# Attention with a gated MLP on one core: the second projection unit of a block placed in the middle of its values unit

## The chip, the cores and the metric

The kernel runs on one NeuronCore of a Trainium2 chip. The metric is the device time of one execution in microseconds (us), as the median of several runs.

## The reference

A layer norm of x (2048 x 640) feeds two branches. The attention branch has 32 heads of width 192 with a K and a V cache of 2048 keys. The other branch is a SwiGLU MLP. The result is x + attention * silu(MLP).

```python
xn = layernorm(x)
q  = (xn @ wq) -> 32 heads of 192
p  = softmax(q @ k_cache.T * 192 ** -0.5)
s  = (p @ v_cache) -> 2048 x 6144, @ wo
g  = silu((silu(xn @ w1) * (xn @ w3)) @ w2)
return x + s * g
```

## The kernel before

Attention ends at 1675 us of the 1976 us profiled. It is a stream of steps. A head has four blocks of 512 queries (`qb`), and a block has eight steps (`p`), each over a pair of 128-key tiles. In each step TensorE does two units of work:

- A scores unit, for the step two ahead: six matmuls of 64 rows and 512 columns, in three pairs: one matmul on the first 64 rows and one on the other 64, which start 20 ns apart in the trace. ACT then takes the exp of the 128 x 1024 result.
- A values unit, for this step: sixteen matmuls of 64 rows and 193 columns, eight pairs, that multiply the exp of two steps ago with V and sum into two output banks.

In two of the eight steps a projection unit for the next head is put in: ten matmuls of 64 rows and 512 columns, five pairs, with a copy on ACT and an add on DVE behind them. The first one (`half` 1, weights `wqB`) stands in step 0, the second one (`half` 0, weights `wq`) in step 4. In head 0, which also computes the layer norm, they stand in steps 5 and 7.

What the argument turns on is PSUM. Scores units and projection units take their output from the same pool, which has two buffers; the output banks have a pool of their own. So each new scores or projection unit needs the buffer of the unit before the last one to have been read.

```python
ps_st = main.enter_context(tc.tile_pool(name="ps_st", bufs=2, space=bass.MemoryType.PSUM))
# ... cut ...
    def project(h, qb, half):
        # ... cut: tiles of the destination ...
        w = L["wqB"] if half else L["wq"]
        ps = ps_st.tile([P, 1024], F32, tag="st2", name="ps")
        # ... cut: head 0 ...
            for c in range(DC):
                for r in range(2):
                    rows = slice(r * 64, (r + 1) * 64)
                    nc.tensor.matmul(ps[:, r * 512:(r + 1) * 512], lhsT=w[rows, c, 0:P], rhs=xnT[rows, c, qs],
                                     start=(c == 0), stop=(c == DC - 1))
            part = hbp.tile([P, 512], F32, tag="part", name="part")
            nc.scalar.copy(out=part[:], in_=ps[:, 0:512])
            nc.vector.tensor_tensor(out=dst, in0=ps[:, 512:1024], in1=part[:], op=ALU.add)
# ... cut ...
    def emit_scores(h, qb, p):
        # ... cut ...
        st2 = ps_st.tile([P, 1024], F32, tag="st2", name="st2")
        # ... cut: three rounds of two matmuls into st2 ...
        pT2 = pp.tile([P, 1024], BF16, tag="pT2", name="pT2")
        nc.scalar.activation(out=pT2[:], in_=st2[:], func=ACT.Exp, scale=att_scale)
# ... cut ...
    for n, (h, qb, p) in enumerate(stream):
        scores(n + 2)
        if h + 1 < H and p == (5 if h == 0 else 0):
            project(h + 1, qb, 1)
        if h + 1 < H and p == (NPAIR - 1 if h == 0 else NPAIR // 2):
            project(h + 1, qb, 0)
        values(n)
        if p == 0 and n > 0:
            finish_block(n - 1)
        if p == (6 if h == 0 else 2) and h < 2 * NPIG:
            swiglu(h, qb)          # even heads: a tanh on ACT and work on DVE; odd heads: DVE alone
```

## Time and profile before

| | before |
|---|---|
| time, median of 3 runs | 1978.36 us |
| TensorE matmul busy | 1952.1 us, 99% of the profiled span |
| ScalarE (ACT) busy | 67% |
| an ordinary step (scores and values) | 1.31 us |
| last score pair to second projection, even heads (64 blocks), median | 360 ns from start to start |
| the same, odd heads (60 blocks), median | 253 ns |
| the same, if nothing waited | 216 ns |

The medians stand for nearly all blocks: four of the even ones, those of head 0, have 267 or 268 ns, two have 530, and one odd block has 216. The second and third rows are from the profile's page. These are its lines of busy time, of the granted clock by slices (in tenths, 9 being 90% or more), and the chain of work that ended last:

```profile
PE 1952.1 (99%) x27311; PEld 1386.0 (70%) x27311; DVE 738.3 (37%) x1109; ACT 1319.6 (67%) x1525; POOL 333.2 (17%) x570
...
PEclk9999999999999999999999999999999999999999
...
PE 96%; ACT 2%; DVE 1%; DMA 1%; issue 0%; ACTq 0%
```

This says that TensorE bounds the kernel, and it seems to say that it never waits. The list of waits agrees on the face of it. It gives the idle time on an engine, who ended it, the total in us, the number of times and the longest:

```profile
PE obank L395 <- ACT osum L405: 2.9, 7, 0.6
...
PE ps L319 <- ACT pT L369: 0.2, 1, 0.2
```

By this list a projection (`ps`, L319) waited for an exp (`pT`, L369) once, for 0.2 us. L319 is the line of both projections. The page's groups of instructions keep them apart (busy us and mean ns of one, then the idle us before them and who ended it):

```profile
L319 PE MATMUL ps<-xnT,wq 64*128 64x512 bf16 x1240 | 155.7, 376 | 0.3
L319 PE MATMUL ps<-xnT,wqB 64*128 64x512 bf16 x1240 | 155.7, 376 | 0.2 <-ACT pT L369 0.2
```

So that one wait belongs to the first projection (`wqB`), and for the second (`wq`) the profile names no wait at all. But a matmul's end is modelled. The Trainium skill, "Perfetto Trace Analysis", Tensor Engine Instruction, says that the profiler estimates it from the instruction's size. Here each 64 x 512 matmul is shown as 376 ns long, while such pairs start 216 ns apart when nothing holds them up. So a wait of up to 160 ns (180 ns after the second matmul of a pair, which starts 20 ns later) lies under the tail of the matmul before it and counts as busy. One has to read starts instead. This is the timeline of the kernel before around one second projection, in an even head (start in us, length in us, engine, source line, operation, tiles, shapes; in brackets the engine's idle time just before):

```profile
804.97 0.62 ACT L345 ACTIVATE pt<-qAB 64x512 bf16<-64x512 bf16 x1
...
805.49 1.00 ACT L369 ACTIVATE pT<-st 128x1024 bf16<-128x1024 f32 x1
...
806.19 0.38 PE L366 MATMUL st<-qC,KC 64*128 64x512 bf16 x1
...
806.55 1.26 PE L319 MATMUL ps<-xnT,wq 64*128 64x512 bf16 x10
...
807.62 0.85 PE L395 MATMUL obank<-vt,pT 64*128 64x193 bf16 x16
807.84 0.58 ACT L322 COPY part<-ps 128x512 f32<-128x512 f32 x1
...
808.46 0.69 DVE L323 TENSOR_TENSOR qAB<-ps,part 128x512 bf16<-128x512 f32 x1 [2.15 <-ACT part L322]
...
809.61 0.38 PE L366 MATMUL st<-qAB,KA 64*128 64x512 bf16 x1
```

The last score pair starts at 806.19 and the projection at 806.55: 360 ns in place of 216. The exp of the scores before (L369) ran from 805.49 to 806.49, and the projection starts just after its end. The distance is 51 or 52 ns in 123 of the 124 blocks, worked out from the starts and lengths in the trace; in the other block nothing waited. The exp is late because the SwiGLU step's tanh (L345, 0.62 us) went ahead of it on ACT. That tanh exists in even heads only. In odd heads the same reading gives 253 ns, again 52 ns after the exp's end, as in this block:

```profile
754.09 1.02 ACT L369 ACTIVATE pT<-st 128x1024 bf16<-128x1024 f32 x1 [0.29 <-PE st L367]
...
754.91 0.38 PE L366 MATMUL st<-qC,KC 64*128 64x512 bf16 x1
...
755.16 1.26 PE L319 MATMUL ps<-xnT,wq 64*128 64x512 bf16 x10
```

The last two lines of the even head's timeline matter for what the change could cost. The projection's buffer is free when the add on DVE is done, at 808.46 + 0.69 = 809.15, and the scores unit that takes it next starts at 809.61, with 455 ns to spare.

### The profile page before, as it was taken

Reading aid. Unit: us, or ns where it says so; the run is one execution under the profiler, and the core shown is the slowest. Engines: PE = TensorE matmul, PEld = TensorE weight load, DVE = VectorE, ACT = ScalarE, POOL = GpSimd, SP = SyncE. Lnnn points to the kernel's source line nnn. Section 1 sums busy time; section 2 is a strip of 40 time slices with the busy share of each in tenths; the row PEclk is TensorE's granted clock in tenths of the full one; section 3 lists DMA queues with packets and bytes.
Section 4 is the critical chain, followed back from the end, with each engine's and each line's share of the span. In section 5 each row is a group of like instructions: output and inputs, shape, how many; then the busy total and the mean of one; then the engine's idle time right before and its main releaser. Section 6 shows DMA issues by size and latency. Waiting matters only on the chain.

```text
span 1976.3 us, 60169 instructions
## 1 busy us (share of the span) xinstructions
PE 1952.1 (99%) x27311; PEld 1386.0 (70%) x27311; DVE 738.3 (37%) x1109; ACT 1319.6 (67%) x1525; POOL 333.2 (17%) x570
## 2 busy tenths in 40 slices
PE   7999999999999999999999999999999999999998
PEld 5677777777777777777777777777777776577776
DVE  5433434333344443334333333443433333521111
ACT  4677787777777777777777777777778777210000
POOL 2222112112221221122122112212211210000000
PEclk9999999999999999999999999999999999999999
DMA  6223233334333434363334343433323230928883
GB/s 153 56 56 91 62 100 66 95 67 100 69 98 69 101 69 99 69 167 67 100 69 101 67 101 69 87 80 73 91 58 92 62 80 4 263 37 150 151 143 70
DMA packets 359718, 177.96 MB, mean 90 GB/s; under 512 B 305552, under 2 KB 346256, under 8 KB 359456
## 3 DMA queue, kind: packets, MB, share of 16 engines
q1 hardware_dynamic: 331824, 113.92, 27.4%
q0 software_dynamic: 23120, 56.72, 11.6%
q8 instruction: 215, 3.52, 0.8%
q10 hardware_dynamic: 4512, 3.41, 0.6%
q14 instruction: 47, 0.39, 0.1%
HBM read 55.44 MB, written 27.79 MB: 42 GB/s over the span
## 4 chain that ended last, share of the span: by engine, by line
PE 96%; ACT 2%; DVE 1%; DMA 1%; issue 0%; ACTq 0%
PE obank L395 34%; PE st L366 30%; PE ps L319 14%; PE ps_s L106 11%; PE st L367 3%; PE ps_f L560 3%; PE ps_gu L531 1%; PE ps_gu L534 1%; ACT pT L369 1%; DMA vt<-in_A_k_cache_dram 1%; PE ps L312 0%; DVE stats L275 0%; ACT osum L405 0%; PE pst L291 0%; ACT xnT L294 0%
## 5 line engine op out<-in xcount | busy, mean ns | idle before, releaser
L369 ACT ACTIVATE pT<-st 128x1024 bf16<-128x1024 f32 x1024 | 1048.9, 1024 | 347.4 <-PE st L367 347.3
L395 PEld LDWEIGHTS <-pT 64*128 64x128 bf16 x16384 | 745.6, 94 | 215.0 <-issue 7.7
L395 PE MATMUL obank<-vt,pT 64*128 64x193 bf16 x16384 | 867.1, 243 | 5.2 <-ACT osum L405 2.9
L366 PE MATMUL st<-qAB,KA 64*128 64x512 bf16 x1024 | 385.1, 376 | 1.6 <-ACT pT L369 0.9
L366 PE MATMUL st<-qC,KC 64*128 64x512 bf16 x1024 | 385.0, 376 | 0.8 <-DVE KC L244 0.8
L366 PE MATMUL st<-qC,KB 64*128 64x512 bf16 x1024 | 385.0, 376 | 0.2 <-ACT qC L329 0.2
L367 PE MATMUL st<-qAB,KA 64*128 64x512 bf16 x1024 | 385.1, 376 | 0.0
L367 PE MATMUL st<-qC,KC 64*128 64x512 bf16 x1024 | 385.0, 376 | 0.0
L367 PE MATMUL st<-qAB,KB 64*128 64x512 bf16 x1024 | 385.0, 376 | 0.0
L332 POOL DMA_DIRECT2D qC<-qAB x254 | 134.4, 529 | 1250.3 <-DVE rl_all L413 654.8
L323 DVE TENSOR_TENSOR qAB<-ps,part 128x512 bf16<-128x512 f32 x248 | 171.4, 691 | 421.8 <-ACT part L322 420.9
L406 DVE COPY opart<-obank 128x772 f32<-128x772 f32 x128 | 123.0, 961 | 425.4 <-PE obank L395 425.4
L106 PE MATMUL ps_s<-wo_sb,oT 128*128 128x256 bf16 (+3 forms) x1536 | 208.8, 299 | 0.0
L106 PEld LDWEIGHTS <-oT 128*128 128x128 bf16 x1536 | 148.4, 98 | 60.4
L366 PEld LDWEIGHTS <-KC 64*128 64x128 bf16 x1024 | 96.2, 94 | 105.1 <-DVE KC L244 1.1
L319 PE MATMUL ps<-xnT,wq 64*128 64x512 bf16 x1240 | 155.7, 376 | 0.3
L319 PE MATMUL ps<-xnT,wqB 64*128 64x512 bf16 x1240 | 155.7, 376 | 0.2 <-ACT pT L369 0.2
L322 ACT COPY part<-ps 128x512 f32<-128x512 f32 x248 | 147.7, 596 | 10.7 <-PE ps L319 0.9
L407 DVE TENSOR_TENSOR osum<-osum,opart 128x772 f32<-128x772 f32 x128 | 123.2, 963 | 21.3 <-ACT osum L405 20.8
L414 DVE TENSOR_TENSOR ostage<-osum,rl_all 128x768 bf16<-128x768 f32 x128 | 122.6, 958 | 4.4
L319 PEld LDWEIGHTS <-wq 64*128 64x128 bf16 x1240 | 67.2, 94 | 77.6 <-issue 26.4
L319 PEld LDWEIGHTS <-wqB 64*128 64x128 bf16 x1240 | 67.2, 94 | 71.4 <-issue 20.0
(75 smaller groups left out, 1263.3 us busy)
## 6 DMA issues: line engine op xcount, KB each, us to landing
vt<-in_A_v_cache_dram SPq DMA_DIRECT2D x32, 768.0 KB, 6.6
o_scr<-ostage SPq DMA_DIRECT2D x16, 1536.0 KB, 8.9
qC<-qAB POOLq DMA_DIRECT2D x381, 64.0 KB, 1.9
wq<-in_A_wq_dram POOLq DMA_DIRECT2D x32, 240.0 KB, 3.5
wo_sb<-in_A_wo_dram POOLq DMA_DIRECT2D x1, 7680.0 KB, 38.5
KC<-KA POOLq DMA_DIRECT2D x31, 128.0 KB, 4.8
KC<-KB POOLq DMA_DIRECT2D x31, 128.0 KB, 5.9
x_all<-in_A_x_dram SPq DMA_DIRECT2D x4, 640.0 KB, 9.3
```

The costliest lines, as they stand in the source:

```text
L106: nc.tensor.matmul(ps[:, 0:w], lhsT=oT[:, k, :], rhs=wo_sb[:, k, c0:c1], start=(k == 0), stop=(k == OC - 1))
L319: nc.tensor.matmul(ps[:, r * 512:(r + 1) * 512], lhsT=w[rows, c, 0:P], rhs=xnT[rows, c, qs], start=(c == 0), stop=(c == DC - 1))
L322: nc.scalar.copy(out=part[:], in_=ps[:, 0:512])
L323: nc.vector.tensor_tensor(out=dst, in0=ps[:, 512:1024], in1=part[:], op=ALU.add)
L332: nc.gpsimd.dma_start(out=qC[0:64, half, qs], in_=qAB[64:P, half, qs])
L366: nc.tensor.matmul(st2[:, 0:512], lhsT=k0, rhs=q0, start=r == 0, stop=r == 2)
L367: nc.tensor.matmul(st2[:, 512:1024], lhsT=k1, rhs=q1, start=r == 0, stop=r == 2)
L369: nc.scalar.activation(out=pT2[:], in_=st2[:], func=ACT.Exp, scale=att_scale)
L395: nc.tensor.matmul(obanks[r][:, j * 256:j * 256 + DH + 1], lhsT=pT2[r * 64:(r + 1) * 64, t * 512 + j * P:t * 512 + (j + 1) * P], rhs=vt[r ...
L406: nc.vector.tensor_copy(out=opart[:], in_=ov[1])
L407: nc.vector.tensor_tensor(out=osum[:], in0=osum[:], in1=opart[:], op=ALU.add)
L414: nc.vector.tensor_tensor(out=ostage[:, qb * 4:qb * 4 + 4, hg * DH:(hg + 1) * DH], in0=osum[:, :, 0:DH], in1=rl.unsqueeze(2).to_broadcast( ...
```

## The change

The intent is to let the second projection unit come later, so that its buffer is free when its turn comes, and to fill the time with half of the values unit, which was ready long before.

```diff
-    def values(n):
+    def values(n, between=None):
@@
         for t in range(2):
+            if t == 1 and between is not None:
+                between()
             for j in range(4):
@@
         if h + 1 < H and p == (NPAIR - 1 if h == 0 else NPAIR // 2):
-            project(h + 1, qb, 0)
-        values(n)
+            values(n, between=lambda: project(h + 1, qb, 0))
+        else:
+            values(n)
```

No instruction is added or removed. In 124 blocks (31 heads of four) eight value matmuls go ahead of the ten projection matmuls. The order on the other engines is the same.

## The prediction

> **What bounds the kernel.** TensorE. The busy table has PE at 99% of the 1976.3 us span, the chain of waits is 96% PE, and the granted clock is full in every slice. But matmul ends are modelled (the Trainium skill, "Perfetto Trace Analysis", Tensor Engine Instruction: the end is an estimate): a 64x512 matmul is shown as 376 ns, while in the timeline such pairs start 215 ns apart. So waits of up to 160 ns are hidden inside "busy", and I read starts instead.
>
> An ordinary step (six score, sixteen value matmuls) takes 1.31 us in the timeline, with a steady 216 ns from the last score pair to the values and 83 ns from one value pair to the next: no waits. At the second projection unit (the one on the plain weights wq) it is not steady. From the last score pair to the first projection pair the starts lie 360 ns apart in 64 of the 124 blocks (even heads) and 253 ns in 60 (odd heads), mean 308, where 216 would be back to back. In every block looked at the projection starts 52 ns after the end of the exp of the step before (806.49 to 806.55 us in one). That is its PSUM wait: scores and projection alternate between two buffers, and the projection needs the one that this exp is reading. In even heads the exp is later because a tanh (0.62 us on ACT) went before it. Matmuls stay in program order, so nothing else runs meanwhile (the Trainium skill, "TensorE: Matmul & The Clock Gate", Part 2, step 1; the trace agrees).
>
> **What the change does.** No instruction is added or removed. Eight value matmuls, ready long before, go in front of the ten projection matmuls; eight stay behind. They take 4 x 83 = 332 ns, so the projection comes no sooner than 548 ns after the last score pair, while its buffer is free at about 360 ns (even) or 253 (odd). The wait goes away.
>
> **Worth.** (308 - 216) ns x 124 = 11.4 us, all of it on PE's chain. The first projection unit (253 ns, 37 ns lost in each of 124 blocks, 4.6 us) is not touched and keeps its wait.
>
> **What could be given back.** The projection ends later against the scores behind it. Its buffer is freed by an ACT copy and a DVE add that end 1.72 us after its last matmul starts. The second scores unit after it takes that buffer; today it starts 455 ns after the add's end. With half the values moved ahead I work out 1.84 us from last projection matmul to that scores unit: 120 ns after the add's end, about 70 after a release of 50. Tight, but it should not wait.  So I expect nothing back.
>
> **Prediction.** 1978.36 - 11.2 = 1967.2 us, range 1965.6 to 1971.0. Within 2%: 0.99.
>
> **What would show it.** Right: in the timeline the first projection pair starts 83 ns after the fourth value pair, in even and odd heads alike; the second values half follows 216 ns after the last projection pair; the first projection unit still shows 253 ns. PE busy falls by about the saving, since the waits were counted as busy.
>
> **What would make it wrong.** If the second scores unit after the projection does wait for the add: each 50 ns there costs 6 us. If changing from 193-column to 512-column matmuls in the middle of the values costs a bubble.

## The result, and the profile after

The changed kernel took 1967.90 us in the median of 4 runs (1967.58 to 1967.97), against 1978.34 us before (the median of 4 runs of its own). That is 10.4 us less: clear of the spread of the runs. The ratio is 0.9948, with a 95% interval of 0.9934 to 0.9962. A ratio here and below is the one for the fast runs of both kernels; it is not quite the ratio of the medians quoted.

The lines of the page after the change that answer to those shown above:

```profile
PE 1942.3 (99%) x27311; PEld 1389.2 (71%) x27311; DVE 738.4 (38%) x1109; ACT 1320.4 (67%) x1525; POOL 333.2 (17%) x570
...
PEclk9999999999999999999999999999999999999999
...
PE 97%; DVE 1%; ACT 1%; DMA 1%; issue 0%; ACTq 0%; DVEq 0%
```

TensorE's busy time fell by 9.8 us, although it executes the same 27311 matmuls. This is the hidden wait leaving the busy time. The share is 99% in both, so it told nothing. This is the timeline after the change, again at a second projection in an even head:

```profile
763.38 1.01 ACT L369 ACTIVATE pT<-st 128x1024 bf16<-128x1024 f32 x1
...
764.08 0.38 PE L366 MATMUL st<-qC,KC 64*128 64x512 bf16 x1
...
764.29 0.51 PE L397 MATMUL obank<-vt,pT 64*128 64x193 bf16 x8
...
764.62 1.26 PE L319 MATMUL ps<-xnT,wq 64*128 64x512 bf16 x10
...
765.70 0.51 PE L397 MATMUL obank<-vt,pT 64*128 64x193 bf16 x8
765.92 0.59 ACT L322 COPY part<-ps 128x512 f32<-128x512 f32 x1 [0.33 <-PE ps L319]
...
766.54 0.69 DVE L323 TENSOR_TENSOR qAB<-ps,part 128x512 bf16<-128x512 f32 x1 [2.34 <-ACT part L322]
...
767.35 0.38 PE L366 MATMUL st<-qAB,KA 64*128 64x512 bf16 x1
```

The exp ends at 764.39, and the projection starts at 764.62, 0.24 us later by the unrounded times, no longer on the exp's heels. Over all 124 blocks the projection starts 83 ns after the value pair ahead of it, in even and odd heads alike, which is the spacing of back-to-back value pairs. The add ends at 766.54 + 0.69 = 767.23, and the next user of the buffer starts at 767.35. The spare time has gone from 455 to 121 ns.

One line of the profile could mislead here. The group of value matmuls is shown 22 us busier after the change (second line) than before (first line):

```profile
L395 PE MATMUL obank<-vt,pT 64*128 64x193 bf16 x16384 | 867.1, 243 | 5.2 <-ACT osum L405 2.9
L397 PE MATMUL obank<-vt,pT 64*128 64x193 bf16 x16384 | 889.1, 243 | 5.6 <-ACT osum L407 3.4
```

The time of a group counts the modelled tail of each run of matmuls. A values unit cut in two has two tails, and 124 more tails of 180 ns each make 22 us. TensorE did not spend that time.

### The profile page after: what moved, and what is told of

Same layout as the page of the kernel before. It is cut to its first block, busy times and chain, and to the rows that moved or that the text cites. A ratio compares the mean times of both kernels' runs of the same rounds, so it can differ in the third digit from the quotient of the medians.

```text
span 1966.1 us, 60169 instructions
## 1 busy us (share of the span) xinstructions
PE 1942.3 (99%) x27311; PEld 1389.2 (71%) x27311; DVE 738.4 (38%) x1109; ACT 1320.4 (67%) x1525; POOL 333.2 (17%) x570
## 4 chain that ended last, share of the span: by engine, by line
PE 97%; DVE 1%; ACT 1%; DMA 1%; issue 0%; ACTq 0%; DVEq 0%
PE obank L397 34%; PE st L366 30%; PE ps L319 14%; PE ps_s L106 11%; PE st L367 3%; PE ps_f L563 3%; PE ps_gu L534 1%; PE ps_gu L537 1%; DMA vt<-in_A_k_cache_dram 1%; ACT pT L369 0%; PE ps L312 0%; DVE stats L275 0%; PE pst L291 0%; PE pk L235 0%; ACT osum L407 0%
## 5 line engine op out<-in xcount | busy, mean ns | idle before, releaser
L397 PE MATMUL obank<-vt,pT 64*128 64x193 bf16 x16384 | 889.1, 243 | 5.6 <-ACT osum L407 3.4
L407 ACT COPY osum<-obank 128x772 f32<-128x772 f32 x128 | 102.0, 797 | 0.9 <-PE obank L397 0.9
```

What stands on the lines that cost most here:

```text
L397: nc.tensor.matmul(obanks[r][:, j * 256:j * 256 + DH + 1], lhsT=pT2[r * 64:(r + 1) * 64, t * 512 + j * P:t * 512 + (j + 1) * P], rhs=vt[r ...
```

## The experiments

Two theories were set against each other. The wait theory is that of the prediction: the projection waits for the exp to leave the buffer, and work put in front fills the wait. The switch theory is the rival: the gap is a cost of going from score matmuls to projection matmuls, and the values in front hide it. Each kernel gave the reference's result. The distances are medians: in head 0's four blocks, which have no such tanh just ahead of the exp, they differ where the projection stands as before (266 to 269 ns).

| run | time, us | ratio to before | last pair to second projection, even / odd heads |
|---|---|---|---|
| before | 1978.3 to 1978.4 | 1 | 360 / 253 ns after scores |
| the change | 1967.90 | 0.9948 | 83 / 83 ns after values |
| tanh moved, no change | 1971.39 | 0.9966 | 252 / 252 ns after scores |
| one value pair ahead | 1971.32 | 0.9965 | 145 / 83 ns after values |
| all eight value pairs ahead | 1998.81 | 1.0104 | 83 / 83 ns after values |
| half the values, then scores, projection | 1968.53 | 0.9950 | 216 / 216 ns after scores |
| six value pairs ahead | 1979.41 | 1.0005 | 83 / 83 ns after values |
| first projection in the middle too | 2051.48 | 1.0370 | 83 / 83 ns after values |
| change, and last scores of a block early | 1962.87 | 0.9921 | 83 / 83 ns after values |
| the same, head 0 as before | 1962.28 | 0.9919 | 83 / 83 ns after values |
| change, and tanh moved | 1967.96 | 0.9948 | 83 / 83 ns after values |

### The tanh moved, the matmuls untouched

This is an edit of the kernel before:

```diff
-        if p == (6 if h == 0 else 2) and h < 2 * NPIG:
+        if p == (6 if h == 0 else 4) and h < 2 * NPIG:
             swiglu(h, qb)
```

> The kernel before, with the order on TensorE untouched; only the SwiGLU step (in even heads a tanh of 0.62 us on ACT) is moved from the block's third step to its fifth, so that it no longer delays the exp that the second projection unit waits for. The wait theory (the projection waits until that exp has left its PSUM buffer): in even heads the projection starts 253 ns after the last score pair in place of 360, as in odd heads; 64 x 107 ns = 6.8 us saved, 1971.5 us. The switch theory (the gap is a cost of going from score matmuls to projection matmuls, and the values in front hide the new weights' load): the order of matmuls is the same, so nothing changes, 1978.3 us.

Measured: 1971.39 us (1970.90 to 1971.71), 7.0 us less than before, and 252 ns in even and odd heads. The same place in an even head:

```profile
764.03 1.02 ACT L369 ACTIVATE pT<-st 128x1024 bf16<-128x1024 f32 x1 [0.29 <-PE st L367]
...
764.85 0.38 PE L366 MATMUL st<-qC,KC 64*128 64x512 bf16 x1
...
765.10 1.25 PE L319 MATMUL ps<-xnT,wq 64*128 64x512 bf16 x10
```

TensorE's order is that of the kernel before, so the part of the gap that goes away with a tanh on another engine was a wait, not a switch. That the sum came to the 6.8 us expected has some luck in it: head 0's four blocks did not shrink, and the two blocks of 530 ns, not counted, made up for them. This leaves the last 37 ns open. They could be either.

### One pair of values in front

```diff
-            if t == 1 and between is not None:
-                between()
             for j in range(4):
+                if t == 0 and j == 1 and between is not None:
+                    between()
```

> As the changed kernel, but only one pair of value matmuls (83 ns) stands in front of the second projection unit, seven behind. The wait theory: the projection comes at 299 ns at the soonest after the last score pair; in odd heads the buffer is free at 253, so no wait; in even heads it is free at 360, so the first projection pair starts about 144 ns after the value pair in place of 83. Saved against before: 64 x 83 + 60 x 37 ns = 7.5 us, 1970.8 us. The switch theory: one pair of values in front hides the switch as well as four do, and 83 ns in all heads, 1967.9 us.

Measured: 1971.32 us (1971.04 to 1971.58). The even heads wait out the rest (145 ns in place of 83, and still 51 ns after the exp's end), and the odd ones do not. In an even head:

```profile
764.28 1.01 ACT L369 ACTIVATE pT<-st 128x1024 bf16<-128x1024 f32 x1
...
765.19 0.26 PE L397 MATMUL obank<-vt,pT 64*128 64x193 bf16 x2
...
765.33 1.25 PE L319 MATMUL ps<-xnT,wq 64*128 64x512 bf16 x10
```

How much must stand in front is set by the exp's end, block by block. The time is half a microsecond over the number expected, about the spread of its runs.

### All the values in front

```diff
-        if h + 1 < H and p == (NPAIR - 1 if h == 0 else NPAIR // 2):
-            values(n, between=lambda: project(h + 1, qb, 0))
-        else:
-            values(n)
+        if h == 0 and p == NPAIR - 1:
+            project(h + 1, qb, 0)
+        values(n)
+        if 0 < h < H - 1 and p == NPAIR // 2:
+            project(h + 1, qb, 0)
```

> The second projection unit behind all sixteen value matmuls of its step (head 0 as before the change). The wait theory with the give-back: the projection itself does not wait, but the second scores unit after it comes 1.51 us after the last projection matmul, and its buffer is free only 1.72 + 0.05 us after it: 260 ns of wait in each of 120 blocks, 31.5 us, less the 11.2 us saved: 1998.6 us, slower than before. A theory without the give-back, where later is as good or better: 1967.5 us.

Measured: 1998.81 us (1998.58 to 1998.90), 20.4 us slower than before. This is its timeline behind a projection:

```profile
778.06 1.26 PE L319 MATMUL ps<-xnT,wq 64*128 64x512 bf16 x10
...
779.35 0.59 ACT L322 COPY part<-ps 128x512 f32<-128x512 f32 x1 [0.66 <-PE ps L319]
...
779.97 0.69 DVE L323 TENSOR_TENSOR qAB<-ps,part 128x512 bf16<-128x512 f32 x1 [2.67 <-ACT part L322]
...
780.72 0.37 PE L366 MATMUL st<-qAB,KA 64*128 64x512 bf16 x1
```

The add ends at 780.66, and the scores unit that takes the buffer starts 52 or 53 ns after the end of the add in every one of the 120 blocks, about 266 ns later than it would have. That is 32 us. So there is a second wait on the other side of the projection, of the same kind, and one cannot move the projection back without limit.

### Half the values, then the scores, then the projection

```diff
-        scores(n + 2)
+        second = h + 1 < H and p == (NPAIR - 1 if h == 0 else NPAIR // 2)
+        if not second:
+            scores(n + 2)
@@
-        if h + 1 < H and p == (NPAIR - 1 if h == 0 else NPAIR // 2):
-            values(n, between=lambda: project(h + 1, qb, 0))
+        if second:
+            values(n, between=lambda: (scores(n + 2), project(h + 1, qb, 0)))
```

> The same eight value matmuls are put ahead, but in front of the scores unit of that step, so that the projection again follows the score matmuls directly. The wait theory: the exp in question has 332 ns more, the projection starts 216 ns after the last score pair in all heads, and the time is that of the changed kernel, 1967.9 us. The switch theory: going from scores to projection costs 37 ns or more again, 253 ns, 124 x 37 ns = 4.6 us more than the changed kernel, 1972.5 us.

Measured: 1968.53 us (1968.00 to 1968.75). The timeline at a projection:

```profile
764.91 0.38 PE L366 MATMUL st<-qC,KC 64*128 64x512 bf16 x1
...
765.13 1.26 PE L319 MATMUL ps<-xnT,wq 64*128 64x512 bf16 x10
```

The projection follows the scores directly, as before the change, and starts 216 ns after them in all 124 blocks. Going from scores to projection takes no longer than going from one pair to the next inside a unit (216 ns), so the 37 ns were a wait too. The switch theory falls. The 0.6 us over the changed kernel are largely a later start: its first score matmul came at 23.3 us in the profiled run, against 22.9 us.

### Six pairs in front

```diff
-            if t == 1 and between is not None:
-                between()
             for j in range(4):
+                if t == 1 and j == 2 and between is not None:
+                    between()
```

> Twelve of the sixteen value matmuls in front of the second projection unit in place of eight (in all heads). The wait theory with the give-back: the second scores unit after it comes 1.68 us after the last projection matmul, and the run with all values in front showed its buffer free 1.775 us after it (the add's end plus 52 ns); 96 ns of wait in 120 blocks, 11.5 us, which gives back all that was saved: 1979.4 us, as before the change. A theory in which any place inside the values is as good: 1967.9 us.

Measured: 1979.41 us (1979.33 to 1980.08), as expected to the tenth. The scores unit waits for the add, 98 ns in each of 120 blocks, and what was saved in front of the projection is lost behind it.

### The first projection in the middle too

```diff
-        if h + 1 < H and p == (5 if h == 0 else 0):
+        if h + 1 < H and p == 0 and h > 0:
+            values(n, between=lambda: project(h + 1, qb, 1))
+            finish_block(n - 1)
+            continue
+        if h == 0 and p == 5:
             project(h + 1, qb, 1)
```

> The changed kernel with the first projection unit placed in the middle of its step's values too (from head 1 on). A simple reading of the wait theory (more work in front fills the wait): 37 ns more saved in each of 120 blocks, 1963.4 us. The full one: that step's values are the first of a block and need the output banks that ACT and DVE are still copying out; in head 31, which has no projection, they wait 730 ns for it in each block; so 120 x (730 - 37) ns = 83 us lost, 2051 us.

Measured: 2051.48 us (2051.22 and 2051.73), 83.6 us over the changed kernel. The first values of a block start 947 ns (the median) after the last score pair in place of 216, since they need output banks that are still being copied out. In the kernel before, the first projection stands exactly in that hole. Where the work that is to be moved ahead has a wait of its own, moving it ahead is a loss.

### The scores of a block's last step early

If the first projection cannot move back, the exp that it waits for can come sooner. That exp belongs to the scores unit that stands in a block's last step (each scores unit works two steps ahead, so this one is for the second step of the next block). It is put into the middle of the values one step earlier:

```diff
-        scores(n + 2)
+        early = h > 0 and p == NPAIR - 2
+        if not (h > 0 and p == NPAIR - 1):
+            scores(n + 2)
@@
             values(n, between=lambda: project(h + 1, qb, 0))
+        elif early:
+            values(n, between=lambda: scores(n + 3))
         else:
```

> The changed kernel, and from head 1 on the scores unit of the step before a block's last is issued half a values unit earlier (the scores of the block's last step go into the middle of the values ahead of it). Its exp, for which the first projection unit of the next block waits, then ends about 0.29 us sooner. The wait theory: the first projection unit starts 216 ns after the last score pair in place of 253 in 119 blocks, 4.5 us; the copy of the output bank on ACT behind that exp also comes 0.29 us sooner, which shortens the 730 ns wait in head 31's four blocks, 1.1 us: 1962.3 us. The switch theory: 253 ns stay, 1967.9 us or 1966.8 us.

Measured: 1962.87 us (1962.69 to 1963.07), 5.0 us less than the changed kernel. This is its timeline at a first projection:

```profile
768.76 0.38 PE L366 MATMUL st<-qC,KC 64*128 64x512 bf16 x1
...
768.98 1.26 PE L319 MATMUL ps<-xnT,wqB 64*128 64x512 bf16 x10
```

From head 1 on, the first projection now starts 216 ns after the last score pair in 119 of the 120 blocks, where it was 253 ns in both the kernel before and the changed one. In head 31 the extra wait of a block's first values fell from 730 ns to between 403 and 442, as the earlier exp lets the copy of the output bank start sooner.

### The same, with head 0 as it was

```diff
-        if h + 1 < H and p == (NPAIR - 1 if h == 0 else NPAIR // 2):
+        if h == 0 and p == NPAIR - 1:
+            project(h + 1, qb, 0)
+        if 0 < h < H - 1 and p == NPAIR // 2:
             values(n, between=lambda: project(h + 1, qb, 0))
```

> The same, with head 0's four blocks as they were before the change (projection in front of the values). In these four the move cost 0.86 us (0.52 us more wait of the first values of a block, 0.34 us more of a projection, both for copies and adds that now come later) and saved 0.2 us. Expected: 0.65 us less than the run with only the early scores, 1961.7 us; if head 0's part of the account is wrong, no difference or a loss.

Measured: 1962.28 us (1962.04 to 1962.69), 0.59 us less in the median, though the two runs' ranges touch. The trace confirms the account: head 0's first values of a block come 618 ns after the last score pair in place of 792 in three blocks, and the one late projection at its end 480 ns in place of 813. A difference of 0.59 us is about the spread of the runs, so the starts carry this point more than the times do. This version beats both kernels, by 16.0 us the one before and by 5.6 us the changed one.

### The change and the moved tanh together

The edit is that of the first experiment, on the changed kernel.

> The changed kernel with the SwiGLU step moved from the block's third step to its fifth as well. Alone, that move saved 7.0 us and the change 10.4 us. The wait theory: both shorten one wait, which the change has already filled entirely, so the exp's sooner end is worth nothing: 1967.9 us. A theory in which they are separate costs and add up: 1961 us.

Measured: 1967.96 us (1967.76 to 1968.31). The two savings do not add up, because they shorten one and the same wait. In the even heads the exp now ends 347 ns before the projection, and nothing comes of it.

## Why the prediction was right

- **The bound.** Predicted: TensorE, with waits hidden in its busy time. Right: busy time fell by 9.8 us with the same instructions. The Trainium skill, "Perfetto Trace Analysis", Identifying the Most-Contended Engine, warns that matmul busy share does not show the distance to the limit. Here 11.4 us of waits stood inside a share of 99%.
- **The wait.** Predicted: the projection waits for the exp that is reading its PSUM buffer, and in even heads longer because of a tanh. Right, and shown from three sides: by taking the tanh away (7.0 us), by giving the exp more time without changing what stands ahead of the projection (216 ns), and by a dose of one pair in front (145 ns in even heads, 83 in odd ones). The trace also has a sign of the wait that needs no modelled end: the two matmuls of the projection's first pair start 5 or 6 ns apart in 123 of the 124 blocks before the change, and 19 or 20 ns apart in all 124 after it. That TensorE cannot pass over the waiting projection is what the Trainium skill says ("TensorE: Matmul & The Clock Gate", Part 2, Step-by-step: matmuls stay in program order). The trace agrees: no values started before the projection, though their exp was done long before.
- **The worth.** Predicted: 11.4 us in front of the projection. In the changed kernel these gaps are all at 83 ns, so that whole sum came. 0.86 us went back in head 0 and 0.4 us within the projection (its first and last pairs start 863 ns apart in place of 860). This leaves 10.1 us; the profiled spans differ by 10.2 us, and 10.4 us were measured. The prediction took 11.2 us off and not its 11.4, without saying where the 0.2 us went; its 1967.2 us was 0.7 us under the time measured.
- **What could be given back.** Predicted: 120 ns left before the scores unit behind, about 70 after the release. Measured: 121 ns, with a release of 52 ns seen in two other kernels. The term was real, as six and eight pairs ahead showed: 98 and 266 ns of wait per block.
- **What was not seen.** "I expect nothing back" was too good by 0.86 us. In head 0 the second projection stands in the last step of a block. There its copy on ACT comes before the copy of the output bank, so the next block's first values start 174 ns later in three blocks. And at the end of head 0 the next user of the projection's buffer is not a scores unit but the first projection of head 1; it already waited for the add before the change (it starts 52 or 53 ns after the add's end in both kernels), and now waits 335 ns longer, once. That is 0.52 + 0.34 us. The step left out was to look at these four blocks apart from the rest: the 120 ns worked out for the buffer's next user hold for the other 120.

The wait in front of the first projection, 37 ns in each block, stayed, as predicted.

## What to carry to other kernels

On a full TensorE, read the distance between starts and compare it with the back-to-back spacing of the same shapes, because waits shorter than the modelled tail are counted as busy and appear in no list of waits. Where a unit waits for a buffer, put work ahead of it that is already able to run, or let the work that frees the buffer come sooner; then follow the moved unit's own buffer to its next user, since the room behind it shrinks as the room in front grows. The best place is an interval that one can work out from a handful of durations: here one pair ahead was too few in half of the blocks, four were safe in all but head 0, and six gave everything back.

## What the Trainium skill lacked or had wrong

- "Perfetto Trace Analysis", Tensor Engine Instruction: it names the propagation of a semaphore, but gives no time for it from one engine to another. From the end of an exp on ACT, or of an add on DVE, to the start of the matmul waiting for it the runs show 50 to 54 ns.
- The same page, Optimization Strategy (consistent bubbles): it speaks of a repeating gap between slices. Here the repeating wait left no gap, because the modelled ends (376 ns) cover it; the page would do well to say that on TensorE one compares starts (here 216 ns from pair to pair of 64-row matmuls of 512 columns, 83 ns for 193).
- "TensorE: Matmul & The Clock Gate", Part 3: it has row tiles starting about 4 ns apart. Here a spacing near that (5 or 6 ns) is seen at the first pair of a projection that had waited. In units that did not wait, nearly all pairs of 64-row matmuls start 19 or 20 ns apart, and the next pair 216 ns after the first.
- The same page, Back-to-back issue gap: it gives about 131 ns per matmul as the sustained figure for 512 columns. Head 0's projections, with all 128 rows, start 215 to 216 ns apart here (225 to 227 for the first gap of three of the eight units), which is the page's figure for a single matmul.
